# An mLSTM cell with a Fourier mixer on one core: who stores the first batch's decays, who splits its maxima, and in which order its states are updated

## The chip, the core and the metric

The kernel runs on one core of a Trainium2 chip (trn2). Time is device microseconds of one execution; lower is better. The engines of the core are TensorE (PE in the profile, its weight loads PEld), VectorE (DVE), ScalarE (ACT), GpSimd (POOL) and SyncE (SP), which here does nothing but issue DMA transfers. Sixteen DMA engines carry all transfers, whoever issued them.

## What is computed

First an mLSTM cell over four batches of eight heads, 768 tokens each, with head dimension 40; then a Fourier mixer with an MLP over rows of 320 features:

```python
for t in range(S):                                  # S = 768, per batch and head
    m_new = maximum(f_gate[t] + m, i_gate[t])
    f_stab, i_stab = exp(f_gate[t] + m - m_new), exp(i_gate[t] - m_new)
    C = f_stab * C + i_stab * outer(v[t], k[t])
    n = f_stab * n + i_stab * k[t]
    y[t] = sigmoid(o_gate[t]) * (C @ q[t]) / maximum(abs(n @ q[t]), 1)
x = y as (4, 768, 320)
u = x + real(fft(fft(x, axis=1), axis=2))
un = (u - mean(u)) / sqrt(var(u) + 1e-6)
out = u + maximum(un @ w_ch1, 0) @ w_ch2
```

## The kernel before, in words

The recurrence is not run token by token. The 768 tokens are six chunks of 128, each of two halves of 64. Within a chunk the products of queries and keys, weighted by exponentials, give what a query takes from its own chunk (`halves_scores`, `mlstm_exp`, `halves_weigh`, `halves_from_chunk`); a state per half gives what it takes from all before (`halves_to_state`, `halves_decay`, `halves_add`, `halves_from_state`).

`gates` works out the running maxima of all 32 pairs of batch and head at once, by scans on VectorE: `sums` and `maxima`, first for chunk 0, then for the other five. `in_order_of_queries` copies the maxima of some chunks into `m` in the order in which the queries lie (chunks 0, 1 and 3 lie backwards). From these come

- `weights`, `columns`, `columns_out`: exponents turned so that tokens lie on partitions (tile `colT`, through TensorE's `pt`);
- `steps`, `steps_out`: the decay of the state per half, `decB`, by a product `pd` out of the tile `dec`;
- `decay`: exponentials `gq` by which queries are scaled. For the first three chunks they are spread over partitions by TensorE (`spread_decay`, tile `pG`); chunks 3 to 5 and the other batches read them back from DRAM: `decay_out` stores them in `G_d`, and `mlstm_load_decay` loads them as `Gb`;
- `spread_max`: the maxima spread over partitions by TensorE (tile `pM`). Chunks 0 and 1 use the fp32 values; for chunks 2 to 5 `parts` splits each maximum into three bf16 parts (`M3`) with copies and subtractions, five operations that depend on each other.

`mlstm_finish` turns a chunk's product into rows of x: five operations on VectorE (tiles `den`, `so`, `x`). The rows of chunks 0, 1 and 3 come out backwards and are moved to their place by DMA (`halves_rows`, `x<-so`). `mix_fold` adds and subtracts pairs of chunks, (2,3), (1,4), (0,5), into `eo` and `fe` for the Fourier products `pz`, `pzt`, `pu`.

There is no scheduler: the program is written out by hand. The beginning of the first batch is a plain list of calls at the end of `gates`. All else is put into slots by `at(slot, phase, function, ...)` and then emitted in order of slot and phase; phases are EVAC 0, FILL 1, MAIN 2, FILL_PE 3. Each engine executes its share of the program in the order in which it was emitted, and waits where an instruction needs another engine's result. `plan_first` places the six chunks of batch 0 three slots apart: chunk c has its scores in slot s = 3c, its product in slot t = s + 3, and the finish after that. `plan_batch` places the mixer and the MLP; `early` places loads. SP issues in program order too: a store that waits for ScalarE holds every load behind it.

`idle_products(n, first)` are TensorE products of zeros that nothing reads. PSUM tiles of one batch rotate over four banks in the order of the string `turn`, one digit for each call of `bank`. `w_ch1` and `w_ch2` come as raw 64-bit floats in pieces of 640 KB (`raw<-in_w`, `Piece.load`), which `take`, `convert` and `join` turn into fp32 (tiles `e`, `m`); three raw buffers rotate.

Of the kernel before, what the change touches and what calls it, by code (L numbers as in the profile page):

```python
# [15 lines left out]
OP = mybir.AluOpType  # L16
# [4 lines left out]
NT = S // L  # L21
# [4 lines left out]
BH = B * H  # L26
# [27 lines left out]
def kernel(  # L54
# [14 lines left out]
    nc = tc.nc  # L69
# [12 lines left out]
    ps_m = pool("ps_m", 1, space=PSUM)  # L82
    scores, heads = (pool(n, 1, space=PSUM).tile([L, 2, NP * L], FP, name=n) for n in ("ps", "ph"))

    turn = iter("321032013013230130123012012301023130201320132013203120123021320321")

    def bank(name, shape, n=None):

# [30 lines left out]
    def at(slot, phase, fn, *args):  # L119
        plan.setdefault((slot, phase), []).append((fn, args))  # L120
# [16 lines left out]
    def gates(gp):  # L137
# [5 lines left out]
        def halves(t):  # L143
            return t.rearrange("p c (i t) -> p c i t", i=2)
# [50 lines left out]
        def maxima(s, initial):  # L195

            c0, c1 = s.start, s.stop
            nc.vector.tensor_tensor(out=a[:, s], in0=a[:, s], in1=F[:, s], op=OP.subtract)
            if c0 > 0:
                nc.vector.tensor_copy(out=shift[:, s, 0:1], in_=F[:, c0 - 1:c1 - 1, L - 1:L])  # L200
            nc.vector.tensor_tensor_scan(out=flat(M, s), data0=flat(shift, s), data1=flat(a, s), initial=initial,
                                         op0=OP.add, op1=OP.max)
            ends = halves(M)[:, s, :, LH - 1]
            nc.vector.tensor_scalar(out=nM[:, s], in0=ends, scalar1=-1.0, scalar2=None, op0=OP.mult)
            nc.vector.tensor_copy(out=m_in[:, s, 1], in_=ends[:, :, 0])
            if c0 > 0:
                nc.vector.tensor_tensor(out=m_in[:, s, 0], in0=M[:, c0 - 1:c1 - 1, L - 1], in1=F[:, c0 - 1:c1 - 1, L - 1],
                                        op=OP.add)

        def in_order_of_queries(eng, c0, c1):  # L210
            out, in_ = (t[:, c0:c1].rearrange("p c (i t) -> p (c i) t", i=2) for t in (m, M))
            eng.tensor_copy(out=out, in_=backwards(in_, LH - 1, LH) if c0 in BACKWARDS else in_)
# [32 lines left out]
                    nc.tensor.matmul(k.M[rows(j), h], w[:, h:h + 1].to_broadcast([w.shape[0], LH]),  # L245
                                     x[:, c, rows(j ^ (h & 1))], start=False, stop=True, skip_group_check=True)

        def parts(c0, c1):

            v, rest_ = m[:, c0:c1], shift[:, c0:c1]  # L250
            nc.gpsimd.tensor_copy(out=M3[0:BH, c0:c1], in_=v)
            nc.gpsimd.tensor_tensor(out=rest_, in0=v, in1=M3[0:BH, c0:c1], op=OP.subtract)
            nc.gpsimd.tensor_copy(out=below[:, c0:c1], in_=rest_)
            nc.gpsimd.tensor_copy(out=M3[BH:2 * BH, c0:c1], in_=rest_)
            nc.gpsimd.tensor_tensor(out=M3[2 * BH:, c0:c1], in0=rest_, in1=below[:, c0:c1], op=OP.subtract)

        def spread_decay(c):
            k, t = chunks[0, c], mlstm_queries(0, c)
# [7 lines left out]
        columns_ = {}  # L266
# [19 lines left out]
        def steps_out():  # L286
            n = [BH, BH // 2, NS - 1]
            v = dv.rearrange("p c i -> p (c i)")[:, 1:]
            nc.vector.tensor_tensor(out=dec, in0=v.unsqueeze(1).to_broadcast(n),
                                    in1=spread_sb[:, L:].unsqueeze(2).to_broadcast(n), op=OP.mult)  # L290
            pd = bank("pd", [L, BH // 2, NS - 1])
            nc.tensor.matmul(pd, spread_sb[:, 0:L], dec, start=True, stop=True)
            nc.vector.tensor_copy(out=decB[:, :, 1:], in_=pd)

        def maxima_out():
            for odd in range(2):
# [2 lines left out]
                                      in_=halves(m)[odd:BH:2, :, i])  # L299

        def decay_out(c0, c1, h0, t=slice(0, L)):
            nc.sync.dma_start(out=G_d[c0:c1, h0:, t].rearrange("c p t -> p c t"), in_=gq[h0:, c0:c1, t])

        first, others = slice(0, 1), slice(1, NT)
        sums(first)
        maxima(first, M_INIT)
        in_order_of_queries(nc.vector, 0, 1)
        columns(0, 1, 0)
        columns_out(0, 1, 0)
        weights(0)  # L310
# [6 lines left out]
        mlstm_exp(0, 0, NP)  # L317
        decay(0)
        mlstm_scale_v(0, 0)
        maxima(others, M[:, 0, L - 1:L])  # L320
        mlstm_load_o(0, 1)
        columns(1, NT, 0)
        in_order_of_queries(nc.vector, 1, 2)
        steps()
        weights(1)
        columns_out(1, NT, 0, nc.vector.tensor_copy)
        for c0, c1, _ in RUNS[1:]:
            in_order_of_queries(nc.gpsimd, c0, c1)
        parts(2, 3)
        spread_max(1)  # L330
        columns(1, 2, 1)
        halves_to_state(0, 0)
        spread_decay(0)
        mlstm_exp(0, 1, 0)
        columns_out(1, 2, 1)
        mlstm_exp(0, 1, NP)
        decay(1)
        halves_weigh(0, 0)
        halves_add(0, 0, 0)
        mlstm_scale_q(0, 0)  # L340
        mlstm_scale_v(0, 1)
        steps_out()
        halves_decay(0, 0, 1)
        weights_of_others()
        halves_add(0, 0, 1)
# [4 lines left out]
                nc.gpsimd.memset(t, 0.0)  # L350

        for s, phase, f, args in (
                (1, FILL, decay, (2,)), (3, FILL + 0.15, parts, (3, 4)), (3, FILL_PE + 4, spread_decay, (1,)),
                (3, FILL_PE + 5, columns, (2, NT, 1)), (4, FILL + 0.3, columns_out, (2, NT, 1)), (1, FILL + 0.1, decay, (3,)),
                (1, FILL + 0.4, decay_out, (1, 4, 0)), (5, FILL + 0.15, parts, (4, 6)), (5, FILL + 0.4, decay, (4,)),
                (5, FILL + 0.5, decay, (5,)), (5, FILL + 0.6, decay_out, (4, 6, 0)),
                (5, FILL + 0.65, decay_out, (0, 1, H, slice(0, LH))), (6, FILL_PE + 4, spread_decay, (2,)),
                (6, FILL + 0.9, maxima_out, ()),
                (7, FILL + 0.5, clear, (fe[:, :, NC:PAD], fe[:, :, PAD + HALF_D - 1:], fe_odd[:, NC:]))):
            at(s, phase, f, *args)  # L360
# [283 lines left out]
    def plan_first():  # L644
        for c in range(NT):
            s = 3 * c
            if c > 1:
                at(s - 2, FILL, mlstm_exp, 0, c, 0)
                at(s - 2, FILL, mlstm_exp, 0, c, NP)
                at(s - 1, FILL, mlstm_scale_v, 0, c)  # L650
            if c > 0:
                at(s + 2 if c < 3 else s, FILL + 0.1, mlstm_scale_q, 0, c)
                at(s, FILL_PE + 2.05, halves_scores, 0, c)
                at(s, FILL_PE + 2.5, halves_to_state, 0, c)
                at(s + 1, FILL - 0.3, halves_weigh, 0, c)
                for i in range(2):
                    at(s + i, FILL + 0.05, halves_decay, 0, c, i)
                    at(s + 1 + i, FILL - 0.2, halves_add, 0, c, i)
            end = c == NT - 1
            t = s + 2 if end else s + 3  # L660
            at(t, FILL_PE, halves_from_state, 0, c)
            at(t, FILL_PE, halves_from_chunk, 0, c, 0)
            at(t, FILL_PE + 0.5, halves_between, 0, c)
            at(t, FILL_PE + 0.6, mlstm_tanh, 0, c)
            at(*((19, FILL_PE) if end else (t, FILL_PE + 3)), halves_from_chunk, 0, c, 1)
            at(20 if end else t + 1, FILL - 0.5, halves_heads, 0, c)
            at(*((21, FILL + 0.05) if end else (17 if c == 4 else t + 1, FILL + 0.3)), mlstm_finish, 0, c)
            if c < 4:
                at(s + 5, FILL - 0.6, halves_rows, 0, c)

    def plan_halves(b, s0, stride=3):
        for c in range(NT):
# [548 lines left out]
    def plan_batch(b, s_mlstm, s_mix, s_mlp):  # L1221
        if b == 0:
            plan_first()
        else:
            plan_halves(b, s_mlstm)
        done = [s_mlstm + n for n in ((16, 19, 22) if b == 0 else (18, 21, 22))]
        assert s_mix >= done[-1] and s_mlp >= s_mix + 9
        late = [s_mlp + 2 * c for c in range(TG)]
        if b == 0:
            feat = [s_mix + 1, s_mix + 1, s_mlp + 3]  # L1230
            turn = [s_mix + 2, s_mix + 3, s_mix + 4]
            add = turn + [s_mlp, s_mlp + 4, s_mlp + 5]
            late = [s_mlp + 2, s_mlp + 5, s_mlp + 7]
        else:
            feat = [s_mix + c for c in ((3, 4, 6) if b == 1 else (3, 4, 7))]
            add = [s_mix + c for c in ((4, 4, 5, 6, 7, 7), (4, 5, 5, 6, 8, 9), (4, 4, 5, 6, 8, 9))[b - 1]]
            turn = [s_mix + c for c in ((5, 6, 6) if b == 1 else (6, 7, 8))]
            late = [s_mix + c for c in ((7, 8, 8) if b == 1 else (9, 10, 10))]
            at(s_mlp, EVAC + 0.5, mlp_sums, 0, 3 if b == 2 else 4)
            if b == 2:  # L1240
                at(s_mlp + 1, MAIN + 0.6, mlp_sums, 3, 4)
        plan_mix(b, s_mix, done, feat, add, turn + late)
        s = s_mlp + NFF + 2
        at(s, FILL + 0.6, mix_rstd, b)
# [19 lines left out]
    for n, (w, p) in enumerate(zip(when, pieces)):  # L1264
        if n > 4:
            at(when[n - 2][2][0] + 1, FILL + 0.7, p.load)
        for (s, phase), fn in zip(w, (p.take, p.convert, p.join)):
            at(s, FILL + phase, fn)

    early = [(3, mlstm_load, 3), (3, mlstm_load_o, 2), (3, mlstm_load_decay, 3), (5, mlstm_load, 4), (6, mlstm_load_o, 3),  # L1270
             (7, mlstm_load_decay, 4), (7, None, 1), (8, mlstm_load, 5), (9, mlstm_load_decay, 5), (9, mlstm_load_o, 4),
             (10, None, 2), (12, load_tables, None), (12, mlstm_load_o, 5), (13, None, 3), (23, None, 4)]
    for s, load, c in early:
        at(s, FILL + 0.8, *((pieces[c].load,) if load is None else (load,) if c is None else (load, 0, c)))
# [121 lines left out]
```

## Time and profile before

| | us |
|---|---|
| median of 3 runs | 408.41 (406.72 to 409.48) |
| the profiled execution | 409.31 |
| its span | 407.3 |
| TensorE busy | 379.7 (93%) |
| VectorE busy | 280.1 (69%) |
| ScalarE busy | 165.6 (41%) |
| GpSimd busy | 135.2 (33%) |
| mean granted TensorE clock | 0.941 |

The profile is of one execution. Busy time is the sum of an engine's instructions; register, branch, semaphore and DMA-issuing instructions are not counted. A row of the timeline gives start, duration, engine, line, operation, output and input tile, count, and in brackets how long the engine had been idle and what released it. "SPq" is the issue of a DMA by SyncE: its duration is the issue's, not the transfer's. In the chain, each piece is the work or the wait that the next piece hung on; "issue" is time in which the engine waited for nothing that the profile shows.

### The profile page before, as it was taken

The page shows a single profiled execution, that of the slowest core. Times are in us where ns is not written, and L with a number is a line of the kernel's source. Part 1 is how long each engine was busy: PE and PEld are TensorE (multiplying, and loading weights), DVE is VectorE, ACT ScalarE, POOL GpSimd, SP SyncE. Part 2 cuts the span into 40 slices and gives each one's busy share as a digit, 9 for nine tenths or more (in the row PEclk, how much of TensorE's full clock was granted, in tenths as well). Part 3 has the DMA queues.
Part 4 walks back from the last instruction along what each step waited for, and adds up shares of the span by engine and source line. Part 5 has one row for each costly group of instructions (what it writes and reads, how often), then busy time and mean ns, then how long its engine had stood idle before and what let it go on. Part 6 is the DMA issues. An engine that isn't in the chain of part 4 may idle for free.

```text
span 407.3 us, 11495 instructions
## 1 busy us (share of the span) xinstructions
PE 379.7 (93%) x4624; PEld 275.8 (68%) x4624; DVE 280.1 (69%) x680; ACT 165.6 (41%) x480; POOL 135.2 (33%) x239
## 2 busy tenths in 40 slices
PE   6868549998999999999999999999999999999996
PEld 4757434555566776766557898956569997556996
DVE  8467459799959958757697479795864786435652
ACT  5563313757654222356355233454550123455000
POOL 5554341266595344318134322471230000020000
PEclk9585558999999999999999999999999999999999
DMA  7367952947869334544850065430000100000000
GB/s 220 104 182 198 353 158 82 238 146 232 235 202 235 93 107 122 160 121 107 215 134 28 16 167 142 137 110 3 0 2 0 35 32 34 0 0 2 32 34 32
DMA packets 25040, 45.31 MB, mean 111 GB/s; under 512 B 5928, under 2 KB 13788, under 8 KB 24860
## 3 DMA queue, kind: packets, MB, share of 16 engines
q1 hardware_dynamic: 24988, 44.59, 38.4%
q8 instruction: 36, 0.59, 0.6%
q14 instruction: 16, 0.13, 0.1%
HBM read 38.49 MB, written 4.12 MB: 105 GB/s over the span
## 4 chain that ended last, share of the span: by engine, by line
PE 67%; DVE 15%; DMA 9%; issue 3%; POOL 2%; ACT 2%; SPq 1%; DVEq 0%; POOLq 0%
PE po L1149 19%; PE pm L1030 14%; PE po L1093 8%; PE pm L968 4%; PE pm L1035 4%; PE ph L504 4%; PE ps L504 3%; DMA qk<-in_qkT 3%; PE pu L847 2%; DMA raw<-in_w 2%; DMA x<-so 2%; DMA kvt<-in_kv 2%; PE pz L804 1%; DVE so L618 1%; PE put L890 1%
## 5 line engine op out<-in xcount | busy, mean ns | idle before, releaser
L1099 DVE SCALAR_TENSOR_TENSOR x<-po,rstd,x 128x160 f32<-128x160 f32 (+1 forms) x69 | 27.1, 394 | 37.1 <-PE po L1149 32.5
L1039 DVE TENSOR_TENSOR h<-h,pm 128x384 f32<-128x384 f32 x60 | 30.5, 549 | 27.2 <-PE pm L1030 12.4
L547 POOL TENSOR_TENSOR C<-C,decB 128x164 f32<-128x164 f32 x40 | 21.8, 546 | 74.8 <-DVE C L562 53.8
L1030 PE MATMUL pm<-uT,w_sb 128*128 128x384 f32 x90 | 37.7, 506 | 1.3 <-DVE uT L1018 0.6
L478 ACT ACTIVATE W<-W,colT 128x64 f32<-128x64 f32 x144 | 37.5, 339 | 0.0
L500 POOL TENSOR_SCALAR_AFFINE_SELECT W<-W 64x512 f32<-64x512 f32 x36 | 27.6, 767 | 25.8 <-ACT W L478 24.4
L1093 PE MATMUL po<-w_sb,h 128*128 128x320 f32 x120 | 34.2, 435 | 0.0
L914 POOL TENSOR_TENSOR t<-rstd 128x6 f32<-128x6 f32 x12 | 3.4, 283 | 79.9 <-DVE v L908 79.4
L968 PE MATMUL pm<-uT,w_sb 128*128 128x384 f32 x80 | 29.2, 500 | 0.1
L1093 PEld LDWEIGHTS po<-w_sb,h 128*128 128x128 f32 x120 | 22.3, 190 | 9.5 <-issue 0.6
L1149 PE MATMUL po<-T,S 128*128 128x160 f32 x180 | 27.8, 301 | 0.3 <-DVE x L1099 0.3
L487 POOL TENSOR_TENSOR qg<-qk,Gb 128x512 f32<-128x512 f32 (+1 forms) x21 | 27.2, 1297 | 0.0
L1149 PEld LDWEIGHTS po<-T,S 128*128 128x128 f32 x180 | 25.5, 190 | 1.7 <-DVE x L1099 0.5
L504 PE MATMUL ph<-kvt,W 64*64 64x41 f32 x768 | 24.7, 244 | 2.0 <-issue 1.2
L1149 PE MATMUL po<-w_sb,h 128*128 128x160 f32 x180 | 26.3, 300 | 0.0
L1149 PEld LDWEIGHTS po<-w_sb,h 128*128 128x128 f32 x180 | 25.2, 190 | 1.4 <-DVE x L1099 0.3
L1030 PEld LDWEIGHTS pm<-uT,w_sb 128*128 128x128 f32 x90 | 15.5, 189 | 15.6 <-DVE h L1039 6.7
L504 PEld LDWEIGHTS ph<-C,qg 40*64 40x64 f32 x704 | 15.7, 151 | 14.8 <-issue 11.2
L567 DVE TENSOR_TENSOR W<-ps,W 128x512 f32<-128x512 f32 x24 | 16.4, 685 | 13.3 <-PE ps L504 10.6
L895 ACT COPY uT<-put 128x384 f32<-128x384 f32 x24 | 11.1, 477 | 31.7 <-PE put L890 31.7
L492 POOL TENSOR_TENSOR vw<-kvt,colT 128x328 f32<-128x328 f32 x24 | 21.3, 889 | 8.1 <-ACT colT L278 6.6
L504 PE MATMUL ph<-C,qg 40*64 40x41 f32 x704 | 18.6, 245 | 5.7 <-DVE qg L485 5.1
(212 smaller groups left out, 832.2 us busy)
## 6 DMA issues: line engine op xcount, KB each, us to landing
kvt<-in_kv SPq DMA_DIRECT2D x24, 336.0 KB
qk<-in_qkT SPq DMA_DIRECT2D x48, 160.0 KB
raw<-in_w SPq DMA_DIRECT2D x10, 640.0 KB
Gb<-G_d SPq DMA_DIRECT2D x36, 128.0 KB
W<-M_d SPq DMA_DIRECT2D x36, 128.0 KB
so<-in_o SPq DMA_DIRECT2D x24, 160.0 KB
out<-x SPq DMA_DIRECT2D x24, 160.0 KB
x<-so SPq DMA_DIRECT2D x12, 140.0 KB
```

What stands on the lines that cost most here:

```text
L478: nc.scalar.activation(out=k.W[:, h, :], in_=x[:, h, :], func=AF.Exp, scale=-1.0, bias=colT[:, c, 0, b * H + h:b * H + h + 1])
L487: nc.gpsimd.tensor_tensor(out=k.qg[:, :, t], in0=k.qk[:, 0, :, t], in1=k.Gb[:, :, t], op=OP.mult)
L492: nc.gpsimd.tensor_tensor(out=k.vw, in0=k.v1, in1=colT[:, c, 1, b * H:(b + 1) * H].unsqueeze(2).to_broadcast([L, H, D1]), op=OP.mult)
L500: nc.gpsimd.affine_select(out=W, in_=W, compare_op=OP.is_ge, fill=0.0, base=base, pattern=[[0, H], [step, LH]], channel_multiplier=-1)
L504: nc.tensor.matmul(out, w, x, start=start, stop=True, skip_group_check=True)
L547: nc.gpsimd.tensor_tensor(out=halves_state(k, i + 1), in0=halves_state(k, i), in1=decB[:, b * NP:(b + 1) * NP, n].unsqueeze(2).to_broadcas ...
L968: nc.tensor.matmul(k.pm[i], w1_sb[:, ch, f0:f0 + L], u[2 * ch], start=(ch == 0 and not ahead), stop=(ch == 1 and ahead), skip_group_check= ...
L1030: nc.tensor.matmul(bank, w, u, start=start, stop=True, skip_group_check=True)
L1039: nc.vector.tensor_tensor(out=h, in0=h, in1=bank, op=OP.add)
L1093: nc.tensor.matmul(k.po[gr, i], hidden(gr, f)[:, i * L:(i + 1) * L], w2_sb[:, f, :], start=(f == 0), stop=(f == NFF - 1))
L1099: nc.vector.scalar_tensor_tensor(out=u, in0=po, scalar=k.rstd[:, c:c + 1], in1=u, op0=OP.mult, op1=OP.add)
L1149: nc.tensor.matmul(po, a[:, f], w[:, f], start=start and f == 0, stop=f == half - 1, skip_group_check=True)
```

## The change

Nine things, all in the first batch:

1. `decay_out` issues its three stores to `G_d` from ScalarE's queue instead of SyncE's.
2. `parts` takes an engine: chunk 2 stays on GpSimd, chunk 3 and chunks 4 and 5 go to VectorE; the latter also one slot later.
3. In `maxima` the maxima of the first chunk of the scan are copied into the order of queries straight after the scan, ahead of `nM` and `m_in`, for chunks 0 and 1.
4. Four idle products are added on TensorE behind the transposes of `columns(1, NT, 0)`, ahead of `spread_max(1)`, with one more digit in `turn`. `columns(1, NT, 0)` is emitted ahead of `maxima(others)`; TensorE's own order is otherwise as it was there.
5. `halves_weigh(0, 0)` and `steps_out()` (the tile `dec` and the product `pd`) are emitted ahead of `halves_to_state(0, 0)`; the copy of `pd` into `decB` becomes `decays_of_chunks`, behind `mlstm_scale_q(0, 0)`.
6. `mlstm_scale_q` of chunks 1 and 2 moves from phase FILL + 0.1 to FILL - 0.15 of its slot, just behind the state additions.
7. `mlstm_finish` of chunks 0 to 3 moves from (t + 1, FILL + 0.3) to (t + 2, FILL - 0.1): behind both state additions of the next chunk.
8. `halves_rows` moves one slot later, and the first fold with it (slot 17 for 16).
9. The raw load of weight piece 1 moves from slot 7 to slot 1.

The order on the engines follows: VectorE runs weighing, both additions, scaled queries and only then the finish of the chunk before; GpSimd runs state decays where the splitting stood; `vw` of chunk 4 stands ahead of GpSimd's two one-row copies of x; on SyncE the loads of qk and kvt of chunk 4 stand ahead of the row moves of chunk 0, and those of chunk 5 ahead of the row moves of chunk 1.

```diff
-    turn = iter("321032013013230130123012012301023130201320132013203120123021320321")
+    turn = iter("3210302031013230130123012012301023130201320132013203120123021320321")
...
             nc.vector.tensor_tensor_scan(out=flat(M, s), data0=flat(shift, s), data1=flat(a, s), initial=initial,
                                          op0=OP.add, op1=OP.max)
+            in_order_of_queries(nc.vector, c0, c0 + 1)
             ends = halves(M)[:, s, :, LH - 1]
...
-        def parts(c0, c1):
+        def parts(eng, c0, c1):
 
             v, rest_ = m[:, c0:c1], shift[:, c0:c1]
-            nc.gpsimd.tensor_copy(out=M3[0:BH, c0:c1], in_=v)
-            nc.gpsimd.tensor_tensor(out=rest_, in0=v, in1=M3[0:BH, c0:c1], op=OP.subtract)
...
+            eng.tensor_copy(out=M3[0:BH, c0:c1], in_=v)
+            eng.tensor_tensor(out=rest_, in0=v, in1=M3[0:BH, c0:c1], op=OP.subtract)
+            eng.tensor_copy(out=below[:, c0:c1], in_=rest_)
+            eng.tensor_copy(out=M3[BH:2 * BH, c0:c1], in_=rest_)
+            eng.tensor_tensor(out=M3[2 * BH:, c0:c1], in0=rest_, in1=below[:, c0:c1], op=OP.subtract)
...
             nc.tensor.matmul(pd, spread_sb[:, 0:L], dec, start=True, stop=True)
-            nc.vector.tensor_copy(out=decB[:, :, 1:], in_=pd)
+            columns_["pd"] = pd
+
+        def decays_of_chunks():
+            nc.vector.tensor_copy(out=decB[:, :, 1:], in_=columns_["pd"])
...
         def decay_out(c0, c1, h0, t=slice(0, L)):
-            nc.sync.dma_start(out=G_d[c0:c1, h0:, t].rearrange("c p t -> p c t"), in_=gq[h0:, c0:c1, t])
+            nc.scalar.dma_start(out=G_d[c0:c1, h0:, t].rearrange("c p t -> p c t"), in_=gq[h0:, c0:c1, t])
...
         maxima(first, M_INIT)
-        in_order_of_queries(nc.vector, 0, 1)
         columns(0, 1, 0)
...
         mlstm_scale_v(0, 0)
+        columns(1, NT, 0)
+        idle_products(4, True)
         maxima(others, M[:, 0, L - 1:L])
         mlstm_load_o(0, 1)
-        columns(1, NT, 0)
-        in_order_of_queries(nc.vector, 1, 2)
         steps()
...
-        parts(2, 3)
+        parts(nc.gpsimd, 2, 3)
         spread_max(1)
         columns(1, 2, 1)
+        halves_weigh(0, 0)
+        steps_out()
         halves_to_state(0, 0)
...
         decay(1)
-        halves_weigh(0, 0)
         halves_add(0, 0, 0)
         mlstm_scale_q(0, 0)
+        decays_of_chunks()
         mlstm_scale_v(0, 1)
-        steps_out()
         halves_decay(0, 0, 1)
...
-                (1, FILL, decay, (2,)), (3, FILL + 0.15, parts, (3, 4)), (3, FILL_PE + 4, spread_decay, (1,)),
+                (1, FILL, decay, (2,)), (3, FILL + 0.15, parts, (nc.vector, 3, 4)), (3, FILL_PE + 4, spread_decay, (1,)),
                 (3, FILL_PE + 5, columns, (2, NT, 1)), (4, FILL + 0.3, columns_out, (2, NT, 1)), (1, FILL + 0.1, decay, (3,)),
-                (1, FILL + 0.4, decay_out, (1, 4, 0)), (5, FILL + 0.15, parts, (4, 6)), (5, FILL + 0.4, decay, (4,)),
+                (1, FILL + 0.4, decay_out, (1, 4, 0)), (6, FILL + 0.15, parts, (nc.vector, 4, 6)), (5, FILL + 0.4, decay, (4,)),
...
-                at(s + 2 if c < 3 else s, FILL + 0.1, mlstm_scale_q, 0, c)
+                at(*((s + 2, FILL - 0.15) if c < 3 else (s, FILL + 0.1)), mlstm_scale_q, 0, c)
...
-            at(*((21, FILL + 0.05) if end else (17 if c == 4 else t + 1, FILL + 0.3)), mlstm_finish, 0, c)
+            at(*((21, FILL + 0.05) if end else (17, FILL + 0.3) if c == 4 else (t + 2, FILL - 0.1)), mlstm_finish, 0, c)
             if c < 4:
-                at(s + 5, FILL - 0.6, halves_rows, 0, c)
+                at(s + 6, FILL - 0.6, halves_rows, 0, c)
...
-        done = [s_mlstm + n for n in ((16, 19, 22) if b == 0 else (18, 21, 22))]
+        done = [s_mlstm + n for n in ((17, 19, 22) if b == 0 else (18, 21, 22))]
...
-    early = [(3, mlstm_load, 3), (3, mlstm_load_o, 2), (3, mlstm_load_decay, 3), (5, mlstm_load, 4), (6, mlstm_load_o, 3),
-             (7, mlstm_load_decay, 4), (7, None, 1), (8, mlstm_load, 5), (9, mlstm_load_decay, 5), (9, mlstm_load_o, 4),
+    early = [(1, None, 1), (3, mlstm_load, 3), (3, mlstm_load_o, 2), (3, mlstm_load_decay, 3), (5, mlstm_load, 4), (6, mlstm_load_o, 3),
+             (7, mlstm_load_decay, 4), (8, mlstm_load, 5), (9, mlstm_load_decay, 5), (9, mlstm_load_o, 4),
```

The three tuples of `decay_out` keep their slots. Tile numbers and line numbers in the new file run one to four higher.

More of the change, by code (lines that the diff above doesn't have):

```diff
@@ L246, in spread_max @@
                                      x[:, c, rows(j ^ (h & 1))], start=False, stop=True, skip_group_check=True)
-        def parts(c0, c1):
+        def parts(eng, c0, c1):
             v, rest_ = m[:, c0:c1], shift[:, c0:c1]
-            nc.gpsimd.tensor_copy(out=M3[0:BH, c0:c1], in_=v)
-            nc.gpsimd.tensor_tensor(out=rest_, in0=v, in1=M3[0:BH, c0:c1], op=OP.subtract)
-            nc.gpsimd.tensor_copy(out=below[:, c0:c1], in_=rest_)
-            nc.gpsimd.tensor_copy(out=M3[BH:2 * BH, c0:c1], in_=rest_)
-            nc.gpsimd.tensor_tensor(out=M3[2 * BH:, c0:c1], in0=rest_, in1=below[:, c0:c1], op=OP.subtract)
+            eng.tensor_copy(out=M3[0:BH, c0:c1], in_=v)
[3 more added lines that the diff above has]
+            eng.tensor_tensor(out=M3[2 * BH:, c0:c1], in0=rest_, in1=below[:, c0:c1], op=OP.subtract)
         def spread_decay(c):
```

## The prediction

> **What bounds the kernel now.** I read the page first (busy shares by slice), then the table by stretches, the chain that ended last, the waits up to 60 us, and the timeline of that stretch. The page's slices are 10.2 us each:
>
> ```profile
> PE   6868549998999999999999999999999999999996
> PEclk9585558999999999999999999999999999999999
> DMA  7367952947869334544850065430000100000000
> ```
>
> From the seventh slice on TensorE is full; only the first six have holes, and there its clock is mostly at half. The stretches say the same (us, busy time of PE, PEld, DVE, ACT, POOL, then clock, DMA share, GB/s):
>
> ```profile
> 14.00:19.00 5.00, 3.87 (x94) 3.18 (x96) 2.73 (x7) 2.05 (x10) 2.20 (x5) 0.50 0.02 6
> ...
> 34.00:55.50 21.50, 13.08 (x387) 10.86 (x383) 8.19 (x20) 6.42 (x26) 6.87 (x10) 0.50 0.93 291
> 100.00:407.30 307.30, 301.72 (x3260) 222.06 (x3258) 209.31 (x529) 116.96 (x322) 89.85 (x161) 1.00 0.31 85
> ```
>
> So from 34 to 55.5 us no engine is the bound; the DMA engines are, at 0.93. After 100 us TensorE is, at 98%. The chain shows where the first batch ends (start, us, what):
>
> ```profile
> 38.63 1.37 SPq L460
> ...
> 40.68 5.71 DMA raw<-in_w
> ...
> 46.41 9.03 DMA x<-so
> ...
> 55.57 0.50 DVE eo L724
> ```
>
> The three x<-so transfers that turn chunk 3's rows are issued at 44.85 and land at 55.45; the first fold (eo, L724) waits for them:
>
> ```profile
> POOL eo L736 <- DMA x<-so: 8.8, 1, 8.8
> DVE eo L724 <- DMA x<-so: 5.0, 1, 5.0
> ```
>
> SyncE's queue shows why they are late (start, us, issue):
>
> ```profile
> 8.34 0.35 SPq L466 DMA_DIRECT2D so<-in_o  x1
> 18.89 0.34 SPq L302 DMA_DIRECT2D G_d<-x  x1
> ...
> 33.26 1.72 SPq L380 DMA_DIRECT2D raw<-in_w  x1
> ...
> 41.79 0.58 SPq L422 DMA_DIRECT2D ds_sb<-in_dft_s  x1
> ...
> 44.85 2.08 SPq L630 DMA_DIRECT2D x<-so  x3
> ```
>
> SP stands from 8.69 to 18.89 before the first store of decays (its row of waits: 9.7 us in one), while the DMA engines work 0.02 of 14 to 19 us; from then to 42.9 it issues without a pause, and everything piles up in front of x<-so. Upstream, chunk 2 shows the other hole:
>
> ```profile
> 26.88 0.66 POOL L255 TENSOR_TENSOR M<-shift,below 32x256 bf16<-32x256 f32 x1
> 27.62 0.46 POOL L547 TENSOR_TENSOR C<-C,decB 128x164 f32<-128x164 f32 x1
> 28.12 0.33 DVE L562 TENSOR_TENSOR C<-C,ps 128x164 f32<-128x164 f32 x1 [1.90 <-POOL C L547]
> ...
> 31.00 0.68 DVE L485 TENSOR_TENSOR qg<-pG,qk 128x512 f32<-128x512 f32 x1
> ...
> 31.83 1.26 PE L504 MATMUL ph<-C,qg 40*64 40x41 f32 x30 [4.61 <-DVE qg L485]
> ```
>
> GpSimd's splitting of the maxima (parts) holds the state's decay, VectorE waits 1.90 us for that, then finishes a chunk (28.36 to 30.85) ahead of the second addition and the scaled queries; TensorE waits 4.61.
>
> **What the Trainium skill says.** TensorE: Matmul & The Clock Gate, Part 1: the clock runs at half until a window of about 3.4 us was busy. The trace agrees: the same 16 pG products took 1.95 us at 20.73 and 1.07 at 26.15. DMA: Bandwidth & Descriptors, Issuing engines are not separate DMA queues: another issuing engine saves only the sequencer's time, the 16 DMA engines stay the same. No ScalarE issue is in this trace; but here the sequencer's standing still is the cost. SBUF — State Buffer, Who interferes with whom: a VectorE operation with two SBUF inputs and a GpSimd one that reads SBUF exclude each other for a whole instruction. The trace agrees: e (L404) took 1.93 us beside GpSimd's 1.27 us qg, 0.82 elsewhere.
>
> **The change part by part.** *Filler products and earlier maxima of chunk 1.* The copy of the maxima goes ahead of nM, m_in, m_in on VectorE, so it ends 0.72 us sooner (9.15 for 9.87). Ahead of the products that need it TensorE now runs four fillers from 7.95: 0.98 each at half clock (the first three: 2.93), about 0.45 to 0.6 at full (one alone took 0.60). That ends at 9.8 to 11.9, then pM L240 0.39 to 0.61 and 32 passes 1.39 to 1.98: 11.6 at full clock, 14.5 at half, against 11.89. So -0.3 to +2.6 here; but the idle 1.72 us, after which the clock was 0.50 until 22.7, is filled. I take full clock as likelier: -0.3, with later products of this stretch shorter.
>
> *State's decays sooner.* W of chunk 0 stood until 13.30 behind ScalarE's colT copies; weighed earlier in the program, it starts at 10.72 and ends 11.4, dec (0.32) at 11.7, pd can run behind the transpose at 11.8 instead of 15.07. GpSimd's first decay then starts when decB is copied, now behind the chunk's qg: about 14.4 (full clock) or 15.7 (half) for 16.45. -2.0 or -0.75. pd's place ahead of ps and pG costs these 0.5 to 0.92, counted in that.
>
> *Parts on VectorE, state additions first.* For (3,4) VectorE has copies of 32x128 at 0.21 and a subtraction at 0.28: 3x0.21+2x0.28 = 1.2 us, where GpSimd took 0.28 to 0.42 each. For (4,6), with 32x640 at 0.81, a subtraction of 256 comes to 0.41 and a copy to 0.33: 1.8. So 3.0 us more on VectorE, 1.75+2.65 off GpSimd. VectorE pays it out of its gaps: 2.59, 1.28, 1.30 and 1.90 us before its four W and C rows. Order after: W, C, C, qg, then the finish (1.65 alone) and the conversion. Walking chunk by chunk with these rows: qg of chunk 1 at 20.0 (full clock) or 22.6 (half) for 23.4; qg of chunk 2 done at 27.0 or 29.6 for 31.68; then finish of chunk 1 (2.3 with GpSimd beside it), the conversion (e, m, join: 1.93+0.81+0.83) and W of chunk 3 at 32.0 or 35.0 for 35.19. So part of the gain is paid back here: that conversion and the moved finish stand in front. Chunk 2's finish ends at 35.8 or 38.8 (before 37.96).
>
> *Decays stored by ScalarE's queue, piece 1 of the weights at slot 1.* SP loses three issues (0.34, 0.52, 0.38) and above all its stand until 18.89: the raw load goes at 8.7, qk of chunk 3 after chunk 0's qg (about 14), where the DMA engines stood idle. Gb of chunk 3 still needs G_d landed, about 20, and is used at 27 or later. ScalarE pays three issues, 0.35 to 0.6 each by SP's rows, up to 1.72 if the ring pushes back as in SP's worst; first behind decays at 17, in front of the chunk's tanh. It has a 5.33 us gap at 28.4. I take 1.3 us, hidden. What was issued at 36.72 (qk of chunk 5) now waits only for chunk 2's qg: 28 to 30.5. The 640 KB of piece 1 leave the crowded stretch (1.9 us at 342 GB/s, the rate of 40 to 50 us).
>
> *Finish and row moves one slot later.* On SP the table loads still stand ahead of chunk 3's row moves. ds_sb is now gated by the 1-row move that waits for GpSimd's copy behind chunk 2's finish: 37.3 or 40.3, for 41.8; I take 39. By then the queue in front is empty, since qk, kvt, Gb, so and raw (1.7 MB) were issued by 35.5. Left in front of the landing: 1155+642+160+640+160 KB = 2757 KB, 2.82 MB: 8.3 us at 342 GB/s. With an estimated 2 us fixed cost (DMA: Bandwidth & Descriptors, Anatomy of one DMA, by its other path; no row here isolates it) x<-so lands at 39+2+8.3 = 49.3 instead of 55.45. Chunk 3's finish must be done by about 44; it is, at 41 to 44. Chunk 4's finish, now ahead of the fold on VectorE, ends at 45 to 50.
>
> *Sum.* Fold, 57.02 us start of pz and all behind it move by 49.3 - 55.45 = -6.2, the finish of chunk 4 (2.3) leaves VectorE's stretch behind the fold, where TensorE is full (57 to 67.7 with one gap, 0.33), so nothing more. Behind that, waits on DMA and VectorE (raw at 67.46, qk after it) hang on the same joins and move along; I take 0 for losses. The profiled run was 409.31 (span 407.3 and 2.0 around): 403.1 there, and the median of before is 408.41: 402.2, said as 402. Ends: ds_sb at 37.3 and 400 GB/s gives -9; ds_sb at 41 gives -4.2.
>
> **The rivals.** *The row moves come early, but another releases the fold* (TensorE's 2.67 us stall "issue" at 46.5, which falls among the table loads again, then heads and finish of chunk 4): fold at 51.2, -4.2, 404.2. For it: that stall is in the trace; against: it lies in a stretch with 3 us of room. *The transfer is merely reordered*: the tables are in front of the rows as before and 291 GB/s stays the limit; then only piece 1's bytes count, 1.9 us, and 406.5. Against: the DMA engines' idle 14 to 19. *Slower: VectorE and GpSimd exclude each other in parts.* Ten dependent operations, each held for a GpSimd instruction of about 1.1 us, cost 14 instead of 3 us on VectorE, 11 more before W of chunk 3, and ds_sb and the rows move by that: +4.8, 413. It decides from 9.2 us (6.2 more than assumed). For it: L404's 1.93; against: GpSimd has less to do there than before, and most parts operations have one SBUF input.
>
> **How the numbers follow.** Main 0.58 (own range 399.5 to 404.5), other release 0.18, reordered 0.13, slower 0.11. Faster by over 1% (about what a measurement of this kernel can tell from no change) means under 404.3: 0.56 of the main case and 0.12 of the second, 0.68. Within 1%: 0.02+0.06+0.13+0.01 = 0.22. Slower: 0.10. The range 398.5 to 407.5 leaves out the slower case and the main case's far ends.
>
> **What would show it.** Right: SP's raw at 8 to 9 us and no stand until 18.9; qg of chunk 2 done by 30; ds_sb at 37 to 40; x<-so landed by 50; pz's start at 50 to 52 instead of 57; the same length from there to the end. Wrong: parts over 5 us in sum, ScalarE rows of G_d over 1 us with heads waiting, pM of chunk 1 ending after 13 us at clock 0.50, or pz early and the end not.

## The result, and the profile after

The changed kernel takes 411.24 us (median of 20 runs, 409.55 to 414.09) beside 409.14 us for the kernel before on the same chip: ratio 1.0064, 95% interval 1.0039 to 1.0089. It is 0.64% slower. The forecast was 402 us, faster. Executions over 1.5% above the fastest of their kernel are left out of the ratios here and below, while the medians take in all.

The profiled execution took 409.55 us, the shortest of the twenty, with a span of 407.8. That is 0.5 us over the span of the profile before, while the medians differ by 2.1 us: this trace shows how the kernel runs, but only a part of its loss. The page's slices, then the table by stretches with the same columns as before:

```profile
PE   8767629998999999999999999999999999999996
PEclk9785558999999999999999999999999999999999
DMA  7834962957967434534850065430000000000000
```

```profile
14.00:19.00 5.00, 4.35 (x145) 3.87 (x144) 3.54 (x10) 2.36 (x12) 2.21 (x3) 0.69 0.66 216
19.00:34.00 15.00, 11.02 (x323) 9.09 (x326) 11.33 (x28) 8.24 (x31) 4.96 (x10) 0.73 0.38 115
34.00:55.50 21.50, 11.88 (x357) 9.99 (x349) 10.53 (x26) 6.25 (x25) 6.95 (x10) 0.50 0.81 267
100.00:407.30 307.30, 302.29 (x3272) 222.64 (x3271) 210.07 (x530) 116.92 (x322) 90.57 (x161) 1.00 0.31 85
```

The hole at 14 to 19 us is filled: DMA share 0.66 for 0.02. But the next 15 us have 0.38, where the kernel before had 0.61:

```profile
19.00:34.00 15.00, 9.88 (x311) 8.38 (x307) 10.53 (x22) 7.69 (x30) 8.79 (x19) 0.73 0.61 162
```

Busy time of the DMA engines from 14 to 34 us is 5 x 0.66 + 15 x 0.38 = 9.0 us, before 5 x 0.02 + 15 x 0.61 = 9.25: in busy time, what was gained in the hole was lost right behind it. In bytes a little was kept, 2.8 MB for 2.5 MB. SyncE's queue shows how (start, us, issue):

```profile
9.76 0.33 SPq L384 DMA_DIRECT2D raw<-in_w  x1
15.78 0.70 SPq L442 DMA_DIRECT2D qk<-in_qkT  x2
16.54 0.35 SPq L444 DMA_DIRECT2D kvt<-in_kv  x1
16.94 0.42 SPq L470 DMA_DIRECT2D so<-in_o  x1
21.77 1.18 SPq L464 DMA_DIRECT2D Gb<-G_d  x2
...
25.67 5.95 SPq L634 DMA_DIRECT2D x<-so  x3
...
36.44 0.85 SPq L442 DMA_DIRECT2D qk<-in_qkT  x2
...
43.69 0.90 SPq L426 DMA_DIRECT2D ds_sb<-in_dft_s  x1
...
46.33 2.04 SPq L634 DMA_DIRECT2D x<-so  x3
```

The stores are now in ScalarE's queue (ACTq):

```profile
18.53 0.36 ACTq L306 DMA_DIRECT2D G_d<-x  x1
...
24.33 1.02 ACTq L306 DMA_DIRECT2D G_d<-x  x2
```

And SyncE's own waits up to 60 us (total, times, longest):

```profile
SPq L442 <- DVE decB L297: 5.7, 1, 5.7
SPq L464 <- DMA G_d<-x: 4.3, 1, 4.3
SPq L634 <- DMA G_d<-x: 3.8, 1, 3.8
```

The single stand of 9.7 us (a time in which SyncE issues nothing) on ScalarE has become three: 5.7 us at L442 until chunk 0's tiles are released (qk of chunk 3, 15.78), 4.3 us for the stored decays to land before they are read back (to 21.77), and 3.8 us inside the row moves of chunk 0. The last is a store of another queue: the three issues grouped as 5.95 us start at 25.67, 30.09 and 31.06, and the second is held until the `G_d` store that ScalarE issued at 24.33 has landed. So qk of chunk 5 is issued at 36.44, hardly sooner than before:

```profile
36.72 0.82 SPq L438 DMA_DIRECT2D qk<-in_qkT  x2
```

The tables go at 43.69 instead of 41.79, chunk 3's rows at 46.33 instead of 44.85. SyncE came to ds_sb at 43.1 and stood a last 0.6 us for the landing of kvt of chunk 5, as the chain that ended last shows:

```profile
37.40 6.28 DMA kvt<-in_kv
43.69 0.90 SPq L426
...
46.33 0.55 SPq L634
...
47.82 8.72 DMA x<-so
```

The fold and the first product of the mixer follow:

```profile
DVE eo L728 <- DMA x<-so: 7.9, 1, 7.9
```

```profile
56.66 0.49 DVE L728 TENSOR_TENSOR eo<-x 128x320 f32<-128x320 f32 x1 [7.94 <-DMA x<-so]
...
58.11 0.98 PE L817 MATMUL pz<-ds_sb,fe 128*128 128x193 f32 x2 [9.40 <-DVE fe L735]
```

The fold is 1.1 us later than before (55.57) and pz too (57.02). From pz to the end it is 349.7 us, before 350.3: in these two executions the loss comes ahead of pz.

### The profile page after: what moved, and what is told of

It reads as the page before. It is cut to its first block, busy times and chain, and to the rows that moved or that the text cites. A ratio compares the mean times of both kernels' runs of the same rounds, so it can differ in the third digit from the quotient of the medians.

```text
span 407.8 us, 11509 instructions
## 1 busy us (share of the span) xinstructions
PE 378.9 (93%) x4632; PEld 275.2 (67%) x4632; DVE 281.7 (69%) x690; ACT 165.5 (41%) x480; POOL 130.7 (32%) x229
## 4 chain that ended last, share of the span: by engine, by line
PE 69%; DVE 11%; DMA 8%; issue 4%; POOL 2%; ACT 2%; SPq 2%; ACTq 0%; POOLq 0%; DVEq 0%
PE po L1153 19%; PE pm L1034 14%; PE po L1097 8%; PE pm L972 6%; DMA kvt<-in_kv 5%; PE ph L508 4%; PE pm L1039 4%; PE pu L851 3%; PE ps L508 3%; DMA x<-so 2%; PE pm L963 2%; PE put L894 1%; PE pz L808 1%; PE pz L820 1%; DMA raw<-in_w 1%
## 5 line engine op out<-in xcount | busy, mean ns | idle before, releaser
L1043 DVE TENSOR_TENSOR h<-h,pm 128x384 f32<-128x384 f32 x60 | 30.5, 548 | 27.2 <-PE pm L1034 12.5
L1090 ACT ACTIVATE h<-h 128x384 f32<-128x384 f32 x45 | 23.1, 520 | 2.0 <-DVE h L1043 2.0
L508 PEld LDWEIGHTS ph<-kvt,W 64*64 64x64 f32 x768 | 19.5, 152 | 6.5 <-issue 3.1
L1039 PE MATMUL pm<-uT,w1t_sb 64*128 64x384 f32 x120 | 23.4, 508 | 0.0
```

Of the source, the lines that this page charges most:

```text
L508: nc.tensor.matmul(out, w, x, start=start, stop=True, skip_group_check=True)
L1039: nc.tensor.matmul(bank, block(w1t_sb, i)[rows], mlp_u(gr, 1)[rows], start=False, stop=True, skip_group_check=True)
L1043: nc.vector.tensor_tensor(out=h, in0=h, in1=bank, op=OP.add)
L1090: nc.scalar.activation(out=h, in_=h, func=AF.Relu, scale=-1.0)
```

## The experiments

Each kernel was run 6 to 22 times. The ratio is to the kernel before on the same chip, whose median stands in the third column; medians from different chips are not compared. "Rows" is the issue of chunk 3's three row moves, "pz" the first product of the mixer, both from the one profiled execution, whose time stands before them. The profile of e9 is of an execution far from its median (413.89 us), so only its times are used.

| run | median us | before there | ratio, 95% interval | profiled us | rows | pz |
|---|---|---|---|---|---|---|
| before | 409.14 | | 1 | 409.31 | 44.85 | 57.02 |
| changed | 411.24 | 409.14 | 1.0064 (1.0039 to 1.0089) | 409.55 | 46.33 | 58.11 |
| e1 | 411.55 | 408.55 | 1.0069 (1.0048 to 1.009) | 410.9 | 45.93 | 57.09 |
| e2 | 410.64 | 408.55 | 1.0037 (1.001 to 1.0063) | 410.01 | 46.01 | 58.95 |
| e3 | 406.58 | 408.55 | 0.9961 (0.9936 to 0.9986) | 406.7 | 45.44 | 54.27 |
| e4 | 409.56 | 408.55 | 1.001 (0.9982 to 1.0039) | 407.84 | 47.88 | 55.73 |
| e5 | 409.06 | 408.78 | 1.0002 (0.998 to 1.0025) | 407.29 | 44.96 | 55.77 |
| e6 | 406.51 | 408.78 | 0.9935 (0.9902 to 0.9969) | 405.6 | 44.71 | 53.17 |
| e7 | 405.9 | 408.78 | 0.9949 (0.9919 to 0.9978) | 403.9 | 45.49 | 53.60 |
| e8 | 406.88 | 408.78 | 0.9924 (0.9897 to 0.9951) | 409.06 | 44.22 | 54.11 |
| e9 | 409.87 | 407.99 | 1.0025 (0.9995 to 1.0054) | | | |
| e10 | 409.77 | 407.99 | 1.0034 (1.0014 to 1.0054) | 407.92 | 44.24 | 56.40 |
| e11 | 405.36 | 407.99 | 0.9912 (0.9889 to 0.9935) | 401.8 | 43.75 | 51.54 |
| e12 | 402.5 | 407.99 | 0.9872 (0.9836 to 0.9908) | 405.09 | 45.40 | 51.02 |
| e13 | 409.33 | 408.41 | 1.0005 (0.9978 to 1.0033) | 409.36 | 44.40 | 55.23 |
| e14 | 410.01 | 408.41 | 1.0046 (1.0025 to 1.0068) | 410.25 | 44.93 | 57.84 |
| e15 | 403.34 | 408.41 | 0.9858 (0.9817 to 0.9898) | 399.8 | 44.40 | 49.24 |

From pz to the end the profiled executions take 348.6 to 353.3 us, without order, so the time of one of them says little. But pz itself goes with the ratios of all runs: it is at 49 to 52 us where the ratio is 0.986 to 0.991, at 53 to 54 for 0.992 to 0.996, and at 55 to 59 for 1.000 and more. When the mixer starts is what tells these kernels apart; the issue of the rows alone, 43.75 to 47.88, does not.

**First set: which of three suspects.** e1 puts the stores back on SyncE, e2 the transposes back behind the subtraction, e3 loads the tables early in the changed kernel, e4 in the kernel before.

```diff
# e1
-            nc.scalar.dma_start(out=G_d[...], ...)
+            nc.sync.dma_start(out=G_d[...], ...)
# e2: columns(1, NT, 0) again behind mlstm_load_o(0, 1)
# e3, e4
-             ... (12, load_tables, None), ...
+    early = [... (1, load_tables, None), ...
```

> The changed kernel with its three stores of decays issued by SyncE again; all else as changed. (As in the changed kernel, the transposes of the gates of chunks 1 to 5 stand ahead of the subtraction, so they turn the gates before it.) Theory A, the stores on ScalarE's queue hold SyncE: in the changed kernel SP stands from 26.3 to 30.1 us at a row move until the second store has landed; that stand goes, the loads of chunk 5 and the tables are issued about 3 us sooner, the fold comes 2 to 3 us sooner, some 408.5 where the changed kernel has 411.2. Theory B, the tables in front of the rows are the bound: SP is quicker, but the rows still wait 8 to 10 us in the DMA queue; within 1 us of the changed kernel. Theory C, VectorE's wait for the transposes: no difference.

> The changed kernel with the transposes of chunks 1 to 5 behind the subtraction again, the four filler products left where they are. Theory C, that wait is the loss: VectorE's subtraction no longer stands 1.31 us, the products of the maxima of chunk 1 start at 9.8 instead of 11.05, the whole first batch 1.3 us sooner, about 410. Theories A and B: the row moves still land at 56 us and the end stays within 0.5 us of the changed kernel.

> The changed kernel with the two table loads (1.8 MB) issued in slot 1, straight behind the early raw piece, instead of slot 12. (The transposes stand ahead of the subtraction, as in the changed kernel.) Theory B: the rows of chunk 3, issued at about 46 us, find an empty queue and land by 49; VectorE's 7.94 us wait for them nearly goes, the fold is at 50 instead of 56.66, the total about 405. Theory A: SP's stand at 26 to 30 stays; gain under 2 us. Rival of both: loads of chunks 3 and 4 come late instead and the engines wait there, no gain.

> The kernel before with the two table loads issued in slot 1, behind the loads of chunk 2's gate, and nothing else of the change. Theory B: the rows of chunk 3, issued near 45 us, land by 48 to 50 instead of 55.45; the fold then waits for TensorE's and ScalarE's work instead, 3 to 5 us sooner: 404 to 406 for 409. Rival, the DMA queue is only rearranged: SP is held by chunk 3's loads being late, within 1 us of the kernel before.

e1 gains nothing. SyncE stands for ScalarE as in the kernel before, and piece 1 stands behind the store:

```profile
SPq L306 <- ACT warm L605: 8.9, 1, 8.9
```

So taking the stores back from ScalarE does not undo the loss; but as SyncE's long stand returns with it, e1 does not test theory A alone. e2 is 0.27% better than the changed kernel, with overlapping intervals: unclear, and its fold is no earlier. e3 is 1.0% better, and its fold waits 4.6 us for rows instead of 7.9. What stands in front of the rows is what counts there. The same edit gives the kernel before nothing (e4): the tables then stand behind the first store, until 18.87 us, piece 1 goes at 38.00, and its rows are issued at 47.88.

**Second set: the finish, and the order of tables and rows.**

```diff
# e5: points 7 and 8 undone (the slot of the first fold not shown)
-            at(*(... else (t + 2, FILL - 0.1)), mlstm_finish, 0, c)
+            at(*(... else (t + 1, FILL + 0.3)), mlstm_finish, 0, c)
-                at(s + 6, FILL - 0.6, halves_rows, 0, c)
+                at(s + 5, FILL - 0.6, halves_rows, 0, c)
# e6 = e3 and e5; e8 = e2, e3 and e5
# e7
-             (10, None, 2), (12, load_tables, None), (12, mlstm_load_o, 5), (13, None, 3), (23, None, 4)]
+             (10, None, 2), (12, mlstm_load_o, 5), (23, None, 4)]
+    at(15, FILL - 0.55, load_tables)          # behind halves_rows of chunk 3
+    at(15, FILL - 0.5, pieces[3].load)
```

> The changed kernel with its points 7 and 8 undone: mlstm_finish of chunks 0 to 3 again at (t + 1, FILL + 0.3), the row moves and the first fold a slot earlier. Theory F (the finish behind both state additions delays chunk 3's rows): SyncE's x<-so of chunk 3 stood for a finish that ended at 45.56; in the old place it ends at 44.8 or before, the three row moves are issued by about 44.5 instead of 46.3, the fold comes 1.5 us sooner, and the time is about 409.5. Theory B (the tables in front of the rows are the bound, whenever the rows are issued): ds_sb is still issued at 42 to 44, the rows land at 55 to 56.5 as before, 411.

> The changed kernel with the tables loaded at slot 1 and, besides, points 7 and 8 undone. With the tables out of the way only the issue of chunk 3's rows is left, at 45.4 to 46.9 there. Theory F: issue by 44, fold at 51 instead of 52.8, 405.0. Theory B alone: the queue in front of the rows (so, raw of piece 2 and 3) decides, same as with tables early alone, 406.6.

> The changed kernel with the two table loads and the raw load of piece 3 placed behind chunk 3's row moves on SyncE instead of ahead of them. Theory B: the rows are then issued at 45 to 46 with 1.8 MB less in front of them and land by 50; the fold follows at 50 to 51, but pz waits for the tables themselves, issued at about 48 and landed at about 53; pz at 53.5 instead of 58.1, 407. If instead the late issue alone is what counts, or the tables merely change places with the rows, pz stays at 57 to 58, 411.

> The changed kernel with tables at slot 1, points 7 and 8 undone, and columns(1, NT, 0) put back behind maxima(others) (fillers kept). If the three losses add up as measured or estimated alone (1.1% for the tables, 0.3% for the transposes, 0.35% for the finish): about 404.5. If they share one cause (the time at which the DMA queue is empty): 406.5, as with tables early alone.

e5 takes back the whole loss: 1.0002 for 1.0064, 0.6% less (0.3 to 1.0 with both intervals combined). So points 7 and 8 together cost it, with all else of the change in place. By which path is not settled. Chunk 3's finish ends at 44.42 instead of 45.56, for it no longer stands behind the additions, and its rows go at 44.96, as theory F has it. But ds_sb goes sooner too, at 40.79 instead of 43.69, and in neither trace did the rows stand for the finish last: SyncE was still issuing the raw piece ahead of them, from 45.58 in the changed kernel, and from 43.56 to 44.85 in e5. The later finish and the later place of the row moves in SyncE's queue were not undone one by one.

e7 is the cleanest look at the queue. The rows are issued no earlier than in e3, but nothing large is in front of them:

```profile
45.49 2.29 SPq L634 DMA_DIRECT2D x<-so  x3
47.82 0.58 SPq L426 DMA_DIRECT2D ds_sb<-in_dft_s  x1
```

```profile
DVE eo L728 <- DMA x<-so: 1.2, 1, 1.2
PE pz L817 <- DVE fe L735: 5.8, 1, 5.8
```

The last row move, issued at 47.24, lands after 1.7 us, where the changed kernel takes 8.7, and the fold starts at 49.03. The prediction had the rows landed at 49.3, but with the tables ahead of them: that the two numbers are near is chance. But pz starts only at 53.60. That it waits for the tables, now behind the rows, fits this trace but is not named there; in e11 it is.

e6 and e8 are 0.26% and 0.37% better than e3, within the intervals. Finish and transposes add little once the tables are early.

**Third set: single parts in the kernel before, and the queue emptied.**

```diff
# e9: before with points 7 and 8; e10: before with points 1 and 9
# e11: before, as e7 (rows are at slot 14 there)
+    at(14, FILL - 0.55, load_tables)
+    at(14, FILL - 0.5, pieces[3].load)
# e12: e6, and pieces 2 and 3 behind the rows
-             (10, None, 2), ... (13, None, 3), ...
+    at(14, FILL - 0.55, pieces[2].load)
+    at(14, FILL - 0.5, pieces[3].load)
```

> The kernel before with points 7 and 8 of the change alone: finish of chunks 0 to 3 behind both state additions, row moves and first fold a slot later. Theory F (this order alone costs what the change lost, about 0.6%): x<-so of chunk 3 issued at 46 to 46.5 instead of 44.85, fold at 56.5 to 57, 411. Rival (it costs only where the rest of the change brings qk and the tables into the same stretch): within 0.2% of before, 409.

> The kernel before with points 1 and 9 alone: the decays' stores on ScalarE's queue and the raw load of piece 1 at slot 1. The prediction gave this part alone the bytes of piece 1 (1.9 us) and an earlier qk of chunk 5 (28 to 30.5 for 36.72): 406.5 or less. The theory formed since (SyncE's stand of 10 us only breaks into others: for G_d's landing, for the completion of the store eight transfers back, for the tiles that chunks release): qk of chunk 5 stays at 35 to 37, rows issued at 44 to 45, 408.5 to 409.

> The kernel before with the tables and the raw load of piece 3 behind chunk 3's row moves. If the place of the tables is worth the same whatever the rest: rows land by 49, pz waits for the tables and starts at 53 to 54 instead of 57.0, 406.5. If the rest of the change is needed for it (as for tables at slot 1, which gave the kernel before nothing, 1.001): 408.5 or more.

> The changed kernel with tables at slot 1, points 7 and 8 undone, and the raw loads of pieces 2 and 3 (first read at about 65 us) behind chunk 3's row moves. If bytes ahead of the rows are what the fold waits for: 1.3 MB less, rows land 2 us after their issue, at 47 to 48, fold and pz at 48.5 to 50 instead of 51.7 and 53.2, 403.5. If the rest of the queue (so, qk of the next batch, the instruction fetches) or TensorE's own products hold pz then, 406.5 as with the tables early and the finish back.

e9 is inconclusive: 0.25%, with an interval that includes nothing and nearly the whole loss. e10 is slower by 0.34%, where the prediction gave this part at least 1.9 us of gain; qk of chunk 5 is issued at 35.58, not at 28 to 30.5. In its profiled execution, one of its shortest, pz is earlier than in the kernel before, though the kernel is slower by the runs: differences under half a per cent are read from the runs, not from one profile.

e11 gains 0.9% in the kernel before, with none of the change. Its 22 times spread from 401.53 to 410.35 us; by the medians of all, 405.36 beside 407.99, it is 0.6%. Now the tables are named:

```profile
PE pz L813 <- DMA ds_sb<-in_dft_s: 2.5, 1, 2.5
```

e12 has tables early and weights late, and is faster than both kernels, by 1.3% than before:

```profile
45.40 2.04 SPq L634 DMA_DIRECT2D x<-so  x3
47.48 1.48 SPq L384 DMA_DIRECT2D raw<-in_w  x2
```

```profile
DVE eo L728 <- DMA x<-so: 1.4, 1, 1.4
```

**Fourth set: what is left of the change, and the same loads without it.**

```diff
# e13: before with points 2 to 6; e14: before with point 1
# e15: before, loads as in e12
+    at(1, FILL + 0.3, load_tables)
+    at(14, FILL - 0.55, pieces[2].load)
+    at(14, FILL - 0.5, pieces[3].load)
-             (10, None, 2), (12, load_tables, None), (12, mlstm_load_o, 5), (13, None, 3), (23, None, 4)]
+             (12, mlstm_load_o, 5), (23, None, 4)]
```

> The kernel before with points 2 to 6 of the change alone (splitting on VectorE, earlier maxima, fillers with the earlier transposes, state's decays sooner, scaled queries ahead); stores, piece 1, finish and row moves as before. The prediction: 3 to 6 us ahead on the engines, and from there an earlier fold: 406 or less. The theory formed since (the fold waits for the row moves, these for the bytes in front of them on the DMA queue, which the engines don't change): x<-so of chunk 3 issued at 44 to 45, fold at 55 to 56, 407.5 to 409.

> The kernel before with point 1 alone: the decays' stores on ScalarE's queue, piece 1 left at slot 7. If the stores by another queue are what costs in points 1 and 9 together (SyncE's later loads and row moves wait for their landing, 3 to 4 us in one stand): 1.003 of before, 409.5. If piece 1 early is (640 KB at 9 to 12 us beside the first batch's own loads): 1.000, 408.

> The kernel before with the tables loaded at slot 1 ahead of the first store of decays (at about 8.7 us) and the raw loads of pieces 2 and 3 behind chunk 3's row moves: the placement of loads of the kernel that ran at 402.5, without any of the change. If the change's lead on the engines counts once the queue is empty: rows issued at 44 to 45 and landed by 47, fold at 47.5 to 50, but chunks 4 and 5 later by their 3 us, 405. If it does not: the same 402.5.

e13: all that moves work between engines brings nothing that can be seen, 1.0005, at most 0.2% by the interval. The rows are issued at 44.40, and VectorE waits 6.3 us for them.

e14: the stores by ScalarE cost 0.46% alone. SyncE's stand of 9.7 us has split as in the changed kernel:

```profile
SPq L438 <- DVE dec L289: 4.9, 1, 4.9
SPq L460 <- DMA G_d<-x: 4.8, 1, 4.8
SPq L438 <- DMA G_d<-x: 2.3, 1, 2.3
```

But its ds_sb goes at 41.78 and its rows at 44.93, as in the kernel before (41.79 and 44.85), so where the 0.46% arise is not shown.

e15: 403.34 us without any of the change, 0.9858, beside 0.9872 for e12 (six runs each). The intervals lie on each other: no worth of points 1 to 6 and 9, which e12 has and e15 has not, can be seen even where the queue in front of the rows is short. Beside e4 two things differ, the tables ahead of the first store and the pieces behind the rows; which of them turns nothing into 1.4% is not separated. Its rows and fold:

```profile
44.40 2.05 SPq L630 DMA_DIRECT2D x<-so  x3
```

```profile
DVE eo L724 <- DMA x<-so: 0.5, 1, 0.5
```

e12 and e15 are the fastest versions, and cannot be told apart.

## Why the prediction was wrong

**The step that failed** is the one on stores and on what SyncE does with the time it gets back: "What was issued at 36.72 (qk of chunk 5) now waits only for chunk 2's qg: 28 to 30.5", and from it "By then the queue in front is empty". It took out the stand of 9.7 us, and let SyncE run on to the next engine's release. In its place SyncE waited 5.7, 4.3 and 3.8 us. The first wait the prediction had (qk of chunk 3 "after chunk 0's qg (about 14)"; it was 15.78). The second was in its hands ("Gb of chunk 3 still needs G_d landed, about 20"), but was read as a bound on when Gb is used, and not as an instruction that stands in SyncE's queue ahead of chunk 4's loads and of the row moves. The third was not foreseen. So qk of chunk 5 went at 36.44 and ds_sb at 43.69, not 39, and the -6.2 of the sum, which hung on this, became +1.1 at the fold. With this part alone in the kernel before, qk of chunk 5 is hardly sooner either (35.58 in e10), and instead of a gain there is a loss (e10, e14).

**The finish and the row moves one slot later** were costed at nothing: "Chunk 3's finish must be done by about 44; it is, at 41 to 44". It ended at 45.56, behind both additions of chunk 4, of which the second waited for GpSimd:

```profile
43.12 0.32 DVE L566 TENSOR_TENSOR C<-C,ps 128x164 f32<-128x164 f32 x1 [0.57 <-POOL C L551]
```

With both undone, the loss is gone (e5), though by which path is open. Alone in the kernel before their cost is not resolved (e9), and the parts do not add up: 0.46% for the stores alone, but nothing visible for stores and piece 1 on top of points 2 to 6 (1.0002 in e5 beside 1.0005 in e13). Why they don't add is left open.

**The rates in front of the rows** were right, the bytes were not. In e7, with little ahead of it, the last row move landed 1.7 us after its issue, near the estimated 2, and in the changed kernel the DMA engines moved 330 GB/s between the issue of ds_sb and the landing, near the assumed 342:

```profile
43.69:56.50 12.81, 4.29 (x144) 3.86 (x136) 4.12 (x11) 2.64 (x11) 2.80 (x3) 0.50 0.95 330
```

But that is 4.2 MB, not 2.82. The queue in front was not empty, for so, a raw piece and a row move had been issued only from 41.40 to 42.55, and the next batch's qk was issued from 48.47, while the rows were still under way. So the rows landed at 56.54, 12.9 us after the issue of ds_sb, and not 10.3: of the 7.2 us between 49.3 and 56.54, 4.7 are the late issue and 2.5 the bytes.

The rival "merely reordered" had this mechanism, the tables ahead of the rows as before; it was wrong in that it still gave a gain for piece 1's bytes. The bytes did move: 6 x 309 + 5 x 216 + 15 x 115 = 4.7 MB between 8 and 34 us, before 6 x 291 + 5 x 6 + 15 x 162 = 4.2 MB. Half a megabyte is 1.6 us at 291 GB/s. That the rows, issued 1.5 us later, cancelled it is likely, but argued. The rival "another releases the fold" was not put to the test, for the rows did not come early.

**Engines.** The parts on VectorE took 3.1 us (predicted 3.0), so the rival "slower" by exclusion is refuted: its sign came true by another path. ScalarE's three issues took 1.38 us (predicted 1.3). GpSimd's first decay came at 16.08 (predicted 14.4 or 15.7, before 16.45). pM of chunk 1 ended at 12.2 us (predicted 11.6 at full clock, before 11.89): the transposes emitted ahead of the subtraction held VectorE, a wait that the prediction did not have:

```profile
7.73 0.81 DVE L198 TENSOR_TENSOR w_sb<-w_sb,F 32x640 f32<-32x640 f32 x1 [1.31 <-PE pt L272]
```

The clock is where much of the engines' part went. It was full to 15.9 us instead of 9.0, but from there on it changed when it had before: half to 22.7, full to 29.6, half to 63.7. So it was half again when the products of chunk 1 came:

```profile
20.72 1.95 PE L264 MATMUL pG<-x,ident 128*64 128x128 f32 x16
...
26.57 0.85 PE L264 MATMUL pG<-x,ident 128*64 128x128 f32 x11
29.58 0.90 PE L264 MATMUL pG<-x,ident 128*64 128x128 f32 x5 [2.17 <-issue]
```

The first row is the 1.95 us of the kernel before, at the same place. So chunk 1's scaled queries ended at 23.41 (predicted 20.0, or 22.6 at half clock, before 23.4): no lead. The Trainium skill, TensorE: Matmul & The Clock Gate, Part 1, gives full clock after a busy window of about 3.4 us and half clock after an idle one. The first agrees with this trace, where TensorE was busy all through the 3.4 us before the clock came back at 22.7. The second does not: in the 10 us of full clock before 15.9 TensorE was never idle for more than 0.86 us at once (until 11.05), and lost full speed all the same.

In chunk 2 a stall of 2.17 us, "issue", cut the products in two: qg of chunk 2 was done at 31.2 (predicted 27.0 or 29.6, before 31.68), W of chunk 3 came at 36.02 (predicted 32.0 or 35.0, before 35.19), chunk 2's finish ended at 39.7 (predicted 35.8 or 38.8, before 37.96). Of the 2 to 4.7 us of lead that were forecast at chunk 2, 0.5 came, and from chunk 3 on the changed kernel was behind. Nor do the engines' points show a worth elsewhere: in e13 the fold waits for the rows all the same, and e15 does without them what e12 does with them.

## What to carry to other kernels

When a stalled load queue is freed, walk every instruction behind it to its own next wait; a transfer's landing holds an in-order queue as firmly as an engine does. If a stage ends on a small transfer, first ask what large transfer stands in front of it that nobody reads yet: moving the two tables ahead and the two pieces of weights behind, three added lines, was worth 1.4% here, and the nine points of the change cost 0.64%. Before a small transfer that a stage ends on, and the operation it waits for, are moved back for the sake of the engines, count what then stands ahead of it in the queue: undoing that took back 0.6% here.

## What the runs showed of the hardware

In this program completions are shared between queues. The trace names, for each transfer, the semaphore that it signals: eight are used in turn, by SyncE's and ScalarE's issues together, and an issue waits until the transfer that had its semaphore before is complete. This is how a store on ScalarE's queue (24.33) held a row move on SyncE's until 30.09. The Trainium skill, DMA: Bandwidth & Descriptors, Issuing engines are not separate DMA queues, says that a second issuing engine saves only the time on the sequencer that issuing takes. In e14 SyncE did not gain even that: its one wait of 9.7 us became waits of 4.9, 4.8 and 2.3 us.

Small stores were slow to complete: 3.2 us after the issue for the first (18.53), with the DMA engines 0.50 busy until then, and 5.8 us for the one at 24.33, with 0.55.

TensorE's "issue" stall of 2.17 us in the changed kernel was 3.5 us in e1, inside the same products. The profile lists a queue of instructions among the DMA queues (36 packets, 0.59 MB); whether the stalls wait for it was not tested.
